# Seven-product units four tiles earlier, with the weight sums moved and the last tile's left half stored on its own

## The chip, the cores and the metric

The kernel runs on one core of one Trainium2 chip. The metric is the time of one launch in device microseconds, as the median of seven runs. TensorE (PE in the profile) multiplies matrices, VectorE (DVE), ScalarE (ACT) and GpSimd (POOL) work element by element, SyncE (SP) issues most transfers. Matrix results arrive in PSUM, in eight banks of 512 fp32 columns for each of 128 partitions; everything else lives in SBUF.

## The reference

Linear attention with a cosine weighting, and then a gated feed-forward block:

```python
# q, k, v: 8 batches x 8 heads x 576 positions x 64
phi(x)  = concat(relu(x) * cos_w, relu(x) * sin_w)            # 128 features
kv      = einsum('bhsf,bhsd->bhfd', phi(k), v)
z       = sum over s of phi(k)
x       = einsum(phi(q), kv) / (einsum(phi(q), z) + 1e-6)     # -> 4608 tokens x 512
out     = (gelu(x @ w_gate) * (x @ w_val)) @ w_out            # 512 -> 1536 -> 512
```

## The kernel before, in words

The 4608 tokens are nine blocks of 512, numbered 0 to 8, and the 1536 hidden columns are twelve tiles of 128 (`JT`). A **unit** is one tile of one block: gate and value for it, the gelu, and the product that gives a tile of `hT`. The attention of batch n + 1 (`kv_unit`, and then five `nm_unit`s that give the numerators and `x_sb`) is spread over the units of block n, and `turn_x` transposes `x_sb` into `xT` by transfers on SyncE's queue.

For blocks 1 to 6 a unit is `gv_unit` (line 401): four matmuls of 128 x 512 for the gate and four for the value, a gelu on ScalarE (line 409) and a multiply on VectorE (line 410). For blocks 7 and 8 it is `fast_unit` (line 602). There gate and value are the two rows of a 2 x 2 block product of W and x, halved along the contraction and along the tokens, and are computed with seven half-size products (`GV`, Winograd's form of Strassen's scheme), each of two matmuls of 128 x 256. It needs four sums of weight blocks, S1 to S4 (`w_sum`, line 566, in slices of 512 columns, 128 x 1024 elements for an instruction), and four sums of x blocks for each block of tokens, T1 to T4 (`x_sum`, line 582). `wa["S1"]` and `wa["S2"]` lie in buffers named `qf`, S3 in `kf`, S4 in `vf`, and the T's in `qp`, whose earlier contents are no longer wanted. In the trace a matmul `ps<-qp,qf` is therefore a product of T and S. Within a unit, product 6 accumulates onto the bank of product 1 and so waits for ScalarE's copy of product 1 (line 631); product 4 accumulates onto product 7's bank and waits for VectorE's reading of it (line 637). Products 7 and 4 of unit t - 1 are issued within unit t.

The output product of block n - 1 runs between the units of block n: it too is in seven products (`product`, line 510, six matmuls of 128 x 256 each), with sums of `hT` blocks (`h_sum`, line 494). VectorE makes these sums up to block 6's units; in the `fast_unit` stretch GpSimd makes them. Each unit of the stretch takes the output step of the unit before it (`o_step`), so the first has none. A finished tile of 128 rows is stored by `store` (line 421) as two transfers of 64 rows.

The order on each engine is the program's order (`tc.manual_schedule()`): an engine stops at an instruction that waits, and all behind it wait too. Before the change the regimes meet at `FAST`, counted in blocks, and the sums have fixed places among the units of block 6:

```python
FAST = NB - 2
W_SUMS = {0: (0,), 1: (1,), 7: (2, 3, 4), 8: (5, 6), 9: (7, 8), 10: (9, 10), 11: (11,)}
...
            if n == FAST - 1:
                for i in W_SUMS.get(jt, ()):
                    w_sum(f"S{i // 3 + 1}", 512 * (i % 3), 512 * (i % 3) + 512)
                if jt >= 8:
                    x_sum(FAST, jt - 8)
```

After the last unit come the output products of block 8's last two tiles of rows, p = 0 and p = 1, in an order written out by hand; the last are product 4 and product 3 of p = 1, which finish the tile `hi` (tokens 384 to 511 of the block) and the right half of `lo` (tokens 128 to 255).

Of the kernel before, what the change touches and what calls it, by code (L numbers as in the profile page):

```python
# [16 lines left out]
def kernel(  # L17
# [13 lines left out]
    nc = tc.nc  # L31

    B, H, S, D = q.shape
    F = 2 * D
    C = H * D
    J = moe_w_gate.shape[1]
    CT = C // 128
    JT = J // 128
    NP = H // 2
    R = S // 64  # L40
    NB = B * S // 512
# [90 lines left out]
    for i in range(2):  # L132
        t = consts.tile([128, NP, R, D + 1], BF16, name=f"vx{i}")
# [282 lines left out]
    def store(engs, i, o_sb, c0=0, c1=C):  # L416

        for n, eng in enumerate(engs):
            b, j = divmod(2 * i + n, R)
            dst = out[b * S:(b + 1) * S, c0:c1].rearrange("(p j) c -> j p c", j=R)[j]  # L420
            eng.dma_start(out=dst, in_=o_sb[64 * n:64 * n + 64, c0:c1])

    def flush(engs=(nc.sync, nc.sync)):
        for i, o_sb in stores:
            store(engs, i, o_sb)
        stores.clear()
# [22 lines left out]
    JH, CH = JT // 2, C // 2  # L449
# [53 lines left out]
    def product(n, p, i, u, m, v):  # L503


        a, b = PROD[i]
        key = n, p
        at = {1: u, 6: u, 7: u, 5: m, 3: m, 2: v, 4: v}[i]
        for j in range(JH):
            nc.tensor.matmul(  # L510
                at,
                lhsT=hs.setdefault(key, h_parts(n, p))[a][:, j],
                rhs=ts[b][:, j],
                start=(j == 0 and i in (1, 2, 4, 5)),
                stop=(j == JH - 1),
                skip_group_check=i in (3, 6, 7),
            )
        if key not in got:
            got[key] = [outp.tile([128, C], FP32, name="o_sb") for _ in range(2)]
        lo, hi = got[key]  # L520
        last = n == NB - 1

        def add(o, k, x, op=ALU.add):
            nc.vector.tensor_tensor(o, got[key, k], x, op=op)  # L524

        if i in (1, 6, 7) or last and i == 5:
            got[key, i] = place(n, p, f"u{i}", CH, FP32)
            nc.scalar.copy(got[key, i], at)  # L528
        if i == (2 if last else 1):
            add(lo[:, LEFT], 1, v)  # L530
        if i == 7:
            add(hi[:, RIGHT], 7, got[key, 5] if last else m)
        if i == 4:
            add(hi[:, LEFT], 7, v, ALU.subtract)
        if i == 3:
            add(lo[:, RIGHT], 6, m)
        if i in (3, 4):
            flush()
            stores.append((4 * n + 2 + p, hi) if i == 4 else (4 * n + p, lo))
            if last:  # L540
                flush((nc.sync, nc.scalar if p == 1 else nc.sync))

# [1 line left out]

    FAST = NB - 2
    CP = CT // 2  # L550
    wa, xb, temps = {}, {}, {}

    def w_sum(name, j0, j1):
        if not wa:
            wa["A11"], wa["A12"] = wg_sb[:, 0:CP], wg_sb[:, CP:CT]
            wa["A21"], wa["A22"] = wv_sb[:, 0:CP], wv_sb[:, CP:CT]
        if name not in wa:
            was = {"S1": "qf", "S2": "qf", "S3": "kf", "S4": "vf"}[name]
            wa[name] = inp.tile([128, CP, J], BF16, name=was)
        x, y, op = {  # L560
            "S1": ("A21", "A22", ALU.add),
            "S2": ("S1", "A11", ALU.subtract),
            "S3": ("A11", "A21", ALU.subtract),
            "S4": ("A12", "S2", ALU.subtract),
        }[name]
        nc.vector.tensor_tensor(  # L566
            wa[name][:, :, j0:j1], wa[x][:, :, j0:j1], wa[y][:, :, j0:j1], op=op
        )

    def x_sum(n, i):  # L570
        if n not in xb:
            xt = xT[n]
            xb[n] = {
                "B11": xt[:, 0:CP, 0:256], "B12": xt[:, 0:CP, 256:512],
                "B21": xt[:, CP:CT, 0:256], "B22": xt[:, CP:CT, 256:512],
            }
        if "x" not in temps:
            temps["x"] = attn.tile([128, 2, 4, CP, 256], BF16, name="qp")
        b = xb[n]
        x, y = (("B12", "B11"), ("B22", "T1"), ("B22", "B12"), ("B21", "T2"))[i]  # L580
        b[f"T{i + 1}"] = temps["x"][:, n - FAST, i]
        nc.vector.tensor_tensor(b[f"T{i + 1}"], b[x], b[y], op=ALU.subtract)  # L582

    GV = {
# [5 lines left out]
    def fast_unit(t, between):  # L590


        def at(i, t):
            if i == 2:
                return ps[:, 0, 256 * (t % 2):256 * (t % 2) + 256]
            return bank((3, 1)[t % 2] if i in (3, 5) else (2, 6, 7)[t % 3])[:, 0:256]

        def mm(i, t):
            n, jt = FAST + t // JT, t % JT
            a, b = GV[i]  # L600
            for ct in range(CP):
                nc.tensor.matmul(  # L602
                    at(i, t),
                    lhsT=wa[a][:, ct, jt * 128:(jt + 1) * 128],
                    rhs=xb[n][b][:, ct],
                    start=(ct == 0 and i in (1, 5)),
                    stop=(ct == CP - 1),
                    skip_group_check=i not in (1, 5),
                )

        def tmp(i, t):
            if "t" not in temps:
                temps["t"] = attn.tile([128, 6, 256], FP32, name="qT")
            return temps["t"][:, 2 * i + t % 2]

        def h(t, half):
            n, jt = FAST + t // JT, t % JT
            if n not in hT:
                hT[n] = ffn.tile([128, JT, BLK], BF16, name="hT")
            return hT[n][:, jt, 256 * half:256 * half + 256]  # L620

        def gelu(t, half, src):
            if t not in gels:
                gels[t] = ffn.tile([128, BLK], FP32, name="gel")
            nc.scalar.activation(gels[t][:, 256 * half:256 * half + 256], src, AF.Gelu)

        new, old = t < 2 * JT, t > 0
        M5, U6, G2 = range(3)
        if new:
            mm(1, t)  # L630
            nc.scalar.copy(at(2, t), at(1, t))  # L631
            mm(5, t)
            nc.scalar.copy(tmp(M5, t), at(5, t))
        if old:
            mm(7, t - 1)
            gelu(t - 1, 1, tmp(G2, t - 1))
            nc.vector.tensor_tensor(at(3, t - 1), tmp(M5, t - 1), at(7, t - 1), op=ALU.add)
            nc.vector.tensor_tensor(
                h(t - 1, 1), gels[t - 1][:, 256:512], at(3, t - 1), op=ALU.mult
            )  # L640
        between()
        if new:
            mm(6, t)
            nc.scalar.copy(tmp(U6, t), at(6, t))
            mm(2, t)
            gelu(t, 0, at(2, t))
            mm(3, t)
            nc.vector.tensor_tensor(tmp(G2, t), tmp(U6, t), at(3, t), op=ALU.add)
        if old:
            mm(4, t - 1)  # L650
            nc.vector.tensor_tensor(
                h(t - 1, 0), gels[t - 1][:, 0:256], at(4, t - 1), op=ALU.mult
            )
# [186 lines left out]
    for n in range(4, 8):  # L840
        SUMS[n] = {0: "1", 1: "23", 2: "4", 3: "5", 4: "6", 5: "7", 6: "8"}

    W_SUMS = {0: (0,), 1: (1,), 7: (2, 3, 4), 8: (5, 6), 9: (7, 8), 10: (9, 10), 11: (11,)}


    q3 = {
# [5 lines left out]
        (2, 1): ((8,), ()),  # L852
    }
    turn[0] = 1
    for n in range(1, FAST):
        b = n + 1

        t_kv, t_nm, t_turn = {1: (7, 9, 12), 2: (6, 7, 11), 3: (2, 5, 9)}.get(n, (1, 2, 8))
        for jt in range(JT):
            if n == 1 and jt >= t_nm:  # L860
                nm_unit(2, jt - t_nm, (6, 4, 6)[jt - t_nm])
                turn_x(2, jt - t_nm)
# [64 lines left out]
                        turn_x(c, i)  # L927
            if n == 1 and 4 <= jt < 8:
                wo_sum(f"T{jt - 3}")
            if n == FAST - 1:  # L930
                for i in W_SUMS.get(jt, ()):
                    w_sum(f"S{i // 3 + 1}", 512 * (i % 3), 512 * (i % 3) + 512)
                if jt >= 8:
                    x_sum(FAST, jt - 8)


    def o_step(n, jt):
        p, u = divmod(jt, 6)
        for i in ((2, 1), (5,), (6,), (7,), (4,), (3,))[u]:
            product(n - 1, p, i, ps[:, 4, 0:CH], ps[:, 5, 0:CH], ps[:, 4, CH:C])  # L940
        for i in map(int, SUMS[n].get(jt, "")):
            h_sum(n - 1, i // 5, f"S{(i - 1) % 4 + 1}", eng=nc.gpsimd)
        if jt % 3 == 1:
            flush()

    for t in range(2 * JT):
        n, jt = FAST + t // JT, t % JT
        if n == NB - 1 and jt in (9, 10):
            h_sum(n, jt - 9, "S3", eng=nc.gpsimd)
        fast_unit(t, lambda: o_step(FAST + (t - 1) // JT, (t - 1) % JT) if t else None)  # L950
        if (n, jt) == (NB - 1, JT - 2):
            for name in ("S1", "S2", "S4"):
                h_sum(n, 0, name, 0, JH - 2, eng=nc.gpsimd)
        if n == FAST and jt in (2, 4, 6, 8):
            x_sum(NB - 1, jt // 2 - 1)

    def last_product(p, i, to=0):
        product(
# [4 lines left out]
        o_step(NB - 1, JT - 1)  # L963
        last_product(0, 1)

    fast_unit(2 * JT, ends)


    for what in (
# [38 lines left out]
```

## Time and profile before

| what | value |
|---|---|
| median of 7 runs | 316.08 us (315.38 to 316.92) |
| the profiled execution's own time | 315.34 us |
| its span | 313.6 us |
| TensorE busy | 303.8 us |
| VectorE, ScalarE, GpSimd busy | 248.0, 183.2, 59.1 us |
| last matmul ends | 308.7 us from the span's start |
| first `fast_unit` matmul | 242.0 us |

The profile is of one execution. Its page gives busy times by engine, then the chain of work that ended last, followed back from the last instruction, and groups of instructions by line with their mean durations. The trace behind it answers for any stretch: a timeline lists start, duration, engine, line and operands, and in brackets the idle time of that engine just before and what ended it. A matmul's duration reaches from its start to its modelled end, and matmuls overlap, so their cost on TensorE is the spacing of starts, which the chain shows.

### The profile page before, as it was taken

Reading aid. Unit: us, or ns where it says so; the run is one execution under the profiler, and the core shown is the slowest. Engines: PE = TensorE matmul, PEld = TensorE weight load, DVE = VectorE, ACT = ScalarE, POOL = GpSimd, SP = SyncE. Lnnn points to the kernel's source line nnn. Section 1 sums busy time; section 2 is a strip of 40 time slices with the busy share of each in tenths; the row PEclk is TensorE's granted clock in tenths of the full one; section 3 lists DMA queues with packets and bytes.
Section 4 is the critical chain, followed back from the end, with each engine's and each line's share of the span. In section 5 each row is a group of like instructions: output and inputs, shape, how many; then the busy total and the mean of one; then the engine's idle time right before and its main releaser. Section 6 shows DMA issues by size and latency. Waiting matters only on the chain.

```text
span 313.6 us, 7631 instructions
## 1 busy us (share of the span) xinstructions
PE 303.8 (97%) x2871; PEld 205.9 (66%) x2871; DVE 248.0 (79%) x610; ACT 183.2 (58%) x452; POOL 59.1 (19%) x64
## 2 busy tenths in 40 slices
PE   8899999999999999999999999999999899999993
PEld 3574456655866676665665666656665688888883
DVE  5864696699897996798697959887889998878782
ACT  7864676957475754366427732683223587777841
POOL 6584420000000000000000000000000951297310
PEclk9999999999999999999999999999999999999999
DMA  7999999861798946984896699365441102113025
GB/s 265 257 183 249 310 320 413 257 151 41 227 216 296 313 97 173 369 183 121 300 294 102 147 323 262 68 120 116 95 92 32 38 10 61 43 27 70 2 68 134
DMA packets 68949, 53.65 MB, mean 171 GB/s; under 512 B 45360, under 2 KB 54064, under 8 KB 68912
## 3 DMA queue, kind: packets, MB, share of 16 engines
q1 hardware_dynamic: 59104, 41.10, 49.7%
q0 software_dynamic: 9648, 11.80, 16.2%
q8 instruction: 22, 0.36, 0.5%
q10 hardware_dynamic: 160, 0.26, 0.2%
q14 instruction: 15, 0.12, 0.1%
HBM read 37.75 MB, written 9.44 MB: 150 GB/s over the span
## 4 chain that ended last, share of the span: by engine, by line
PE 90%; DVE 4%; DMA 3%; issue 1%; SPq 1%; ACT 0%; DVEq 0%
PE ps L401 44%; PE ps L510 23%; PE ps L602 11%; PE ps L431 3%; PE ps L283 3%; PE ps L242 3%; DMA vf<-in_v_dram 3%; DVE qp L582 1%; PE ps L205 1%; PE ps L373 1%; PE ps L358 1%; SPq L81 1%; DVE o_sb L524 0%; DVE vf L566 0%; DVE hT L410 0%
## 5 line engine op out<-in xcount | busy, mean ns | idle before, releaser
L401 PE MATMUL ps<-xT,wg_sb 128*128 128x512 bf16 (+1 forms) x360 | 85.6, 360 | 0.0
L401 PE MATMUL ps<-xT,wv_sb 128*128 128x512 bf16 (+1 forms) x360 | 85.6, 360 | 0.0
L409 ACT ACTIVATE gel<-ps 128x512 f32<-128x512 f32 (+1 forms) x90 | 50.2, 559 | 51.1 <-PE ps L401 44.5
L410 DVE TENSOR_TENSOR hT<-gel,ps 128x512 bf16<-128x512 f32 (+1 forms) x90 | 56.9, 636 | 26.2 <-PE ps L401 21.3
L401 PEld LDWEIGHTS <-wv_sb 128*128 128x128 bf16 x360 | 35.2, 98 | 35.8
L494 POOL TENSOR_TENSOR S<-hT 128x768 bf16<-128x768 bf16 x8 | 13.3, 1663 | 212.1 <-DVE hT L410 199.0
L401 PEld LDWEIGHTS <-wg_sb 128*128 128x128 bf16 x360 | 32.3, 98 | 21.9 <-issue 0.2
L510 PEld LDWEIGHTS <-S 128*128 128x128 bf16 x336 | 32.9, 98 | 11.5 <-DVE S L494 0.7
L528 ACT COPY u<-ps 128x256 f32<-128x256 f32 x42 | 15.6, 372 | 33.5 <-PE ps L510 33.0
L510 PE MATMUL ps<-T,S 128*128 128x256 bf16 x252 | 34.4, 273 | 0.0
L161 ACT ACTIVATE qp<-qf,sin_t 128x256 bf16<-128x256 f32 x72 | 32.1, 502 | 2.0 <-DMA qf<-in_q_dram 2.0
L510 PEld LDWEIGHTS <-hT 128*128 128x128 bf16 x288 | 28.2, 98 | 7.1
L524 DVE TENSOR_TENSOR o_sb<-u,ps 128x256 f32<-128x256 f32 x56 | 23.4, 417 | 12.0 <-ACT u L528 11.5
L161 ACT ACTIVATE kp<-kf,sin_t 128x256 bf16<-128x256 f32 (+1 forms) x73 | 30.0, 480 | 0.9 <-DMA kf<-in_k_dram 0.9
L296 DVE TENSOR_TENSOR x_sb<-ps,rec 128x512 bf16<-128x512 f32 x38 | 26.3, 691 | 1.7 <-DMA xT<-x_sb 0.4
L510 PE MATMUL ps<-wo_sb,hT 128*128 128x256 bf16 x192 | 23.7, 273 | 0.0
L163 DVE TENSOR_SCALAR qp<-qf,cos_t 128x256 bf16<-128x256 f32 x71 | 21.6, 351 | 2.7 <-DMA qf<-in_q_dram 2.7
L602 PE MATMUL ps<-qp,qf 128*128 128x256 bf16 x96 | 18.3, 272 | 0.3 <-ACT ps L631 0.3
L602 PE MATMUL ps<-xT,wg_sb 128*128 128x256 bf16 x96 | 18.3, 273 | 0.0
L163 DVE TENSOR_SCALAR kp<-kf,cos_t 128x256 bf16<-128x256 f32 x63 | 18.3, 348 | 0.0
L283 PEld LDWEIGHTS <-qT 128*128 128x128 bf16 x304 | 14.6, 98 | 2.6 <-ACT qT L698 0.3
L283 PE MATMUL ps<-kv_sb,qT 128*128 128x65 bf16 x304 | 16.1, 194 | 0.0
(117 smaller groups left out, 416.1 us busy)
## 6 DMA issues: line engine op xcount, KB each, us to landing
out_dram<-o_sb SPq DMA_DIRECT2D x70, 128.0 KB, 2.4
kf<-in_k_dram SPq DMA_DIRECT2D x12, 576.0 KB, 6.9
vf<-in_v_dram SPq DMA_DIRECT2D x12, 576.0 KB, 8.9
qf<-in_q_dram SPq DMA_DIRECT2D x10, 576.0 KB, 4.9
qf<-in_q_dram POOLq DMA_DIRECT2D x4, 576.0 KB, 12.2
kf<-in_k_dram POOLq DMA_DIRECT2D x4, 576.0 KB, 12.6
vf<-in_v_dram POOLq DMA_DIRECT2D x4, 576.0 KB, 12.7
wg_sb<-in_moe_w_gate_dram POOLq DMA_DIRECT2D x6, 256.0 KB, 6.1
```

What stands on the lines that cost most here:

```text
L161: nc.scalar.activation(o, i, AF.Relu, scale=tab[:, j:j + 1])
L163: (eng or nc.vector).tensor_scalar(o, i, 0.0, tab[:, j:j + 1], op0=ALU.max, op1=ALU.mult)
L283: nc.tensor.matmul(bank(b0 + h // 4)[:, (h % 4) * (D + 1):(h % 4 + 1) * (D + 1)], lhsT=q_cols(b, t, h), rhs=kv_sb[b][:, h // 2, h % 2, :], ...
L296: nc.vector.tensor_tensor(x, nm[:, :, :, 0:D], rec[:, :, :, None].to_broadcast([128, 2, 4, D]), op=ALU.mult,)
L401: nc.tensor.matmul(bank(b0 + g)[:, 0:w], lhsT=wt[:, ct, js], rhs=xt[:, ct, c0:c0 + w], start=(ct == 0), stop=(ct == CT - 1),)
L409: nc.scalar.activation(gel[:, 0:w], bank(b0)[:, 0:w], AF.Gelu)
L410: nc.vector.tensor_mul(hT[n][:, jt, c0:c0 + w], gel[:, 0:w], bank(b0 + 1)[:, 0:w])
L494: eng.tensor_tensor(a[name][:, j0:j1], a[x][:, j0:j1], a[y][:, j0:j1], op=op)
L510: nc.tensor.matmul(at, lhsT=hs.setdefault(key, h_parts(n, p))[a][:, j], rhs=ts[b][:, j], start=(j == 0 and i in (1, 2, 4, 5)), stop=(j == ...
L524: nc.vector.tensor_tensor(o, got[key, k], x, op=op)
L528: nc.scalar.copy(got[key, i], at)
L602: nc.tensor.matmul(at(i, t), lhsT=wa[a][:, ct, jt * 128:(jt + 1) * 128], rhs=xb[n][b][:, ct], start=(ct == 0 and i in (1, 5)), stop=(ct == ...
```

## The change

The boundary is now counted in units: the last four units of block 6 (8 to 11) are done by `fast_unit` as well, 28 of them instead of 24. During these four the output step keeps its own unit's place, and the first unit of block 7 has no output step; from then on each takes the step of the unit before, as it was.

The W sums are split by columns. Those for columns 1024 to 1535, which the four new units use, and all of S1 and S3 are made by VectorE, from block 5 on. The first two thirds of S2 and S4 are made by GpSimd, 128 x 1024 elements for an instruction, after a copy of one element of block 7's T4 into `gate`; the copy stands ahead of them in GpSimd's order. The x sums of block 6 (new) go to its units 3 to 6, those of block 7 to its unit 7, those of block 8 to units 8 to 11 of block 7. In block 6 the remaining transposes of x go to unit 7 instead of unit 8.

In the last tile pair (p = 1 of block 8), the left half of `lo` is stored after product 2, by two transfers on SyncE's queue; `hi` after product 4, on SyncE's and GpSimd's; the right half of `lo` after product 3, on SyncE's and ScalarE's. Before, `hi` and the whole of `lo` were stored on SyncE's and ScalarE's queues. The pending stores are flushed once more after the last unit.

```diff
-        if i in (3, 4):
+        if last and p == 1:
+            if i == 2:
+                store((nc.sync, nc.sync), 4 * n + p, lo, 0, CH)
+            if i == 4:
+                store((nc.sync, nc.gpsimd), 4 * n + 2 + p, hi)
+            if i == 3:
+                store((nc.sync, nc.scalar), 4 * n + p, lo, CH, C)
+        elif i in (3, 4):
             flush()
             stores.append((4 * n + 2 + p, hi) if i == 4 else (4 * n + p, lo))
             if last:
-                flush((nc.sync, nc.scalar if p == 1 else nc.sync))
+                flush()
...
-    FAST = NB - 2
+    FAST = (NB - 3) * JT + 8
+    UNITS = NB * JT - FAST
...
-    def w_sum(name, j0, j1):
+    def w_sum(name, j0, j1, eng=nc.vector):
...
-        nc.vector.tensor_tensor(
+        eng.tensor_tensor(
...
-        b[f"T{i + 1}"] = temps["x"][:, n - FAST, i]
+        b[f"T{i + 1}"] = temps["x"][:, n % 2, i]
...
-    W_SUMS = {0: (0,), 1: (1,), 7: (2, 3, 4), 8: (5, 6), 9: (7, 8), 10: (9, 10), 11: (11,)}
+    MORE = {
+        (5, 0): [("S1", 0, 512)], (5, 1): [("S1", 512, 1024)],
+        (5, 8): [("S3", 0, 512)], (5, 9): [("S3", 512, 1024)],
+        (6, 0): [("S1", 1024, J), ("S2", 1024, J)],
+        (6, 1): [("S3", 1024, J)], (6, 2): [("S4", 1024, J)],
+        (6, 3): [(6, 0)], (6, 4): [(6, 1)], (6, 5): [(6, 2)], (6, 6): [(6, 3)],
+        (6, 7): [(7, 0), (7, 1), (7, 2), (7, 3)],
+        (7, 8): [(8, 0)], (7, 9): [(8, 1)], (7, 10): [(8, 2)], (7, 11): [(8, 3)],
+    }
+
+    def more(n, jt):
+        for what in MORE.get((n, jt), ()):
+            (w_sum if len(what) == 3 else x_sum)(*what)
...
-    for n in range(1, FAST):
+    for n in range(1, NB - 2):
...
+        if n == 6:
+            t_turn = 7
-        for jt in range(JT):
+        for jt in range(min(JT, FAST - n * JT)):
...
-    for t in range(2 * JT):
-        n, jt = FAST + t // JT, t % JT
+    for t in range(UNITS):
+        n, jt = divmod(FAST + t, JT)
...
-        fast_unit(t, lambda: o_step(FAST + (t - 1) // JT, (t - 1) % JT) if t else None)
+        if n < NB - 2:
+            fast_unit(t, lambda: o_step(n, jt))
+            if t == 0:
+                nc.gpsimd.tensor_copy(gate, xb[NB - 2]["T4"][:, CP - 1, 255:256])
+            a, j0 = (("S2", 0), ("S4", 0), ("S2", 512), ("S4", 512))[t]
+            w_sum(a, j0, j0 + 512, eng=nc.gpsimd)
+        elif (n, jt) == (NB - 2, 0):
+            fast_unit(t, lambda: None)
+        else:
+            fast_unit(t, lambda: o_step(*divmod(FAST + t - 1, JT)))
+        more(n, jt)
...
-    fast_unit(2 * JT, ends)
+    fast_unit(UNITS, ends)
+    flush()
```

More of the change, by code (lines that the diff above doesn't have):

```diff
@@ L616, in h @@
         def h(t, half):
-            n, jt = FAST + t // JT, t % JT
+            n, jt = divmod(FAST + t, JT)
             if n not in hT:
@@ L625, in gelu @@
             nc.scalar.activation(gels[t][:, 256 * half:256 * half + 256], src, AF.Gelu)
-        new, old = t < 2 * JT, t > 0
+        new, old = t < UNITS, t > 0
         M5, U6, G2 = range(3)
@@ L929 @@
                 wo_sum(f"T{jt - 3}")
[L930 to L934, printed above, removed]
+            more(n, jt)
     def o_step(n, jt):
@@ L944, in o_step @@
             flush()
-    for t in range(2 * JT):
-        n, jt = FAST + t // JT, t % JT
+    for t in range(UNITS):
+        n, jt = divmod(FAST + t, JT)
         if n == NB - 1 and jt in (9, 10):
             h_sum(n, jt - 9, "S3", eng=nc.gpsimd)
-        fast_unit(t, lambda: o_step(FAST + (t - 1) // JT, (t - 1) % JT) if t else None)
+        if n < NB - 2:
[8 more added lines that the diff above has]
+            fast_unit(t, lambda: o_step(*divmod(FAST + t - 1, JT)))
+        more(n, jt)
         if (n, jt) == (NB - 1, JT - 2):
@@ L953 @@
                 h_sum(n, 0, name, 0, JH - 2, eng=nc.gpsimd)
-        if n == FAST and jt in (2, 4, 6, 8):
-            x_sum(NB - 1, jt // 2 - 1)
     def last_product(p, i, to=0):
```

## The prediction

> **What bounds the kernel now.** I read the page's busy table, the chain that ended last, then the timelines of each engine around the change from full products to seven products, the groups by form, and the stores at the end. A unit is one column tile (0 to 11) of a block of 512 tokens (0 to 8); t counts seven-product units.
>
> ```profile
> PE 303.8 (97%) x2871; PEld 205.9 (66%) x2871; DVE 248.0 (79%) x610; ACT 183.2 (58%) x452; POOL 59.1 (19%) x64
> PE 90%; DVE 4%; DMA 3%; issue 1%; SPq 1%; ACT 0%; DVEq 0%
> ```
>
> TensorE bounds it: only fewer matmul slots, fewer gaps, or a shorter end can move the time. The chain, in order of time (start, us, what):
>
> ```profile
> 232.66 1.73 PE ps L401 x8
> ...
> 245.09 1.85 DVE qp L582
> ...
> 249.63 1.53 PE ps L602 x14
> 251.16 0.66 PE ps L510 x6
> ```
>
> A full unit is 8 matmuls in 1.73 us, a seven-product unit 14 in 1.53; six matmuls of the output product (0.66 or 0.65) stand between. Between the two regimes the chain leaves TensorE for VectorE. The timelines of PE, DVE and POOL there:
>
> ```profile
> 242.90 0.38 PE L602 MATMUL ps<-qp,qf 128*128 128x256 bf16 x2 [0.28 <-ACT ps L631]
> ...
> 247.85 0.38 PE L602 MATMUL ps<-qp,wv_sb 128*128 128x256 bf16 x2 [1.52 <-DVE ps L637]
> ```
>
> ```profile
> 243.13 2.03 DVE L566 TENSOR_TENSOR vf<-wg_sb,qf 128x1024 bf16<-128x1024 bf16 x1
> 245.09 1.85 DVE L582 TENSOR_TENSOR qp<-xT,qp 128x512 bf16<-128x512 bf16 x1
> ```
>
> ```profile
> 242.98 1.63 POOL L494 TENSOR_TENSOR S<-hT 128x768 bf16<-128x768 bf16 x1 [199.04 <-DVE hT L410]
> 244.69 1.96 POOL L494 TENSOR_TENSOR S<-S,hT 128x768 bf16<-128x768 bf16 x1
> ```
>
> The reader sees two sums on VectorE three to four times their usual length (the same forms take 0.69 and 0.42 us), exactly while GpSimd sums, and TensorE waiting behind them. The bracketed idle understates it, since the last matmul's drain counts as busy. I count slots: from 242.02 (first seven-product matmul) to 251.65 there are 44 matmuls of gate and value and 24 of output, 68 x 0.109 = 7.42 us, in 9.63 us. **The change of regime costs 2.21 us**: 0.44 at the first wait, 1.68 at the second, 0.09 after it.
>
> [...] the sums above grew by 1.34 and 1.43 us, while the operations that take one input from PSUM stayed at 0.42 us beside the same GpSimd sums. [...] The stores here land after 2.2 to 3.0 us; no small store from GpSimd is in this trace.
>
> **Part 1, four more units in seven products.** Units 8 to 11 of block 6: 32 matmuls at 0.216 (6.91 us) become 56 at 0.109 (6.12): **-0.79 us**, all on the path, since TensorE has no idle there. Beside it ScalarE gets five 0.36 to 0.43 us operations a unit for one of 0.60, and VectorE four of 0.42 for one of 0.68. The existing seven-product stretch carries just that beside gapless TensorE, so it costs nothing; without that cover each late VectorE step would hold fourth products as at 247.85.
>
> **Part 2, the sums.** Twelve W sums of 0.69 us ran on VectorE in block 6; now eight run there from block 5 on, four on GpSimd. One more set of four x sums (0.42 each, about 0.35 apart) is added for block 6. I laid these into VectorE's timeline. Block 5, units 8 and 9: +1.2 us, into idle pieces of 1.33 and 0.66 us; unit 0 of block 6 gets two W sums for one (+0.6), into 1.52 us of idle before unit 2's multiply. Units 3 to 6 get one x sum each, so a unit needs 0.60 + 0.33 + 0.47 + 1.05 + 0.35 = 2.8 us against 2.64 on TensorE: VectorE falls behind by up to 0.8 us and catches up in the 0.95 us of idle before 230.46. The tightest place is the numerators: their banks 6 and 7 must be read before the next eight matmuls. Those at 226.72 follow an x_sb which ended at 226.25 and would end at 226.6: 0.1 us to spare. Cost taken 0, bounds 0 and +0.5; it cannot be below 0, as there is no idle there to win. Block 7's four x sums follow unit 7's multiply, 233.3 to 234.9.
>
> GpSimd's four sums are held by a one-element copy from the last of these, so they meet no two-SBUF-input operation of VectorE: during t = 0 to 3 its operands come from PSUM and one SBUF tile. No 128x1024 sum on GpSimd is in the trace; the rows by form are
>
> ```profile
> L494 POOL TENSOR_TENSOR S<-hT 128x768 bf16<-128x768 bf16 x8 | 13.3, 1663 | 212.1 <-DVE hT L410 199.0 <-PE ps L602 12.5 <-PE ps L510 0.6
> L494 POOL TENSOR_TENSOR kf<-hT 128x512 bf16<-128x512 bf16 x1 | 1.2, 1154 | 4.9 <-DVE hT L638 4.9
> ```
>
> The unstretched 1.64 and 1.15 us give 1.9 ns an element, so 2.1 us for 1024. From 235.1 they end at 237.2, 239.4, 241.5 and 243.7. Unit t starts at 232.5 + 2.19 t: S2's first half is needed at 241.9, S4's at 242.3, the second halves four units later. Queued behind them on GpSimd is the first sum S1 of block 6's h, whose last operand comes at about 243.6; it ends at 245.3 and is needed at 246.5. Cost taken 0; with the worst stretch seen (1.96/1.63) a sum is 2.6 us and that product waits 0.6. Bounds 0 and +0.6.
>
> **Part 3, the change of regime.** The 2.21 us go, as no VectorE sum overlaps a GpSimd one and block 7's x sums are done ten microseconds before use. At t = 0 the six output matmuls now stand ahead of product 6 and cover ScalarE's copy. At t = 4 (unit 0 of block 7) nothing does: only product 7 of the unit before precedes, so product 6 issues 0.66 us after the unit's start where the copy is done at 0.88 (242.02 to 242.90 before). That leaves 0.22: **-1.99 us** (bounds -2.2 and -1.4). The transposes of block 8's x move one unit earlier in SyncE's queue, past no store that delays anyone: 0.
>
> **Part 4, the end.** The last stores' issues (start, us):
>
> ```profile
> 309.15 0.54 SPq L421 DMA_DIRECT2D out_dram<-o_sb  x1
> 309.25 0.73 ACTq L421 DMA_DIRECT2D out_dram<-o_sb  x1
> ```
>
> Both carry 128 KB and follow VectorE's last add (308.70 to 309.12). Now they carry 64 KB, ScalarE's queue no longer issues the other tile's half before (about 0.1 us), and 128 KB less are moved in all[...]. The left half's two issues go earlier, at about 301 us, ahead of two stores of the first tile that nobody waits for. In exchange half a tile goes through GpSimd at about 305.8: 0.7 to 0.8 us to issue (its load rows) for 0.56[...], so it lands about when the last one does. Taken **-0.3 us**; bounds -0.7 and +0.3.
>
> **Sum.** -0.79 - 1.99 - 0.30 = -3.1 us. The profiled execution took 315.34 us (span 313.6 and 1.74 around it), so 312.2, with a span of 310.5 and the last matmul ending near 305.9 instead of 308.7. That execution lies 0.74 under the median of 316.08; the median becomes **313.0 us**.
>
> **Rivals.** (A) VectorE becomes the bound: the numerators' 0.1 us is not enough, or the four x sums of block 7 push t = 0's work, so that stalls of 1 to 2 us come back in block 6. For it: a demand of 2.8 against 2.64 us. Against: 0.95 us of idle right after. Half the gain or less, 314.5 us. (B) Slower: GpSimd paces the start of block 7. If a W sum takes d, the four end at 235.1 + 4d and S1 1.64 later, needed at 246.5: every 0.1 us of d beyond 2.44 costs 0.4 us. From d = 3.2 the whole gain is gone; at 3.6 TensorE loses 4.6 us, net +1.5, 317.6. For it: the size isn't in the trace and strides over two runs of 512. Against: the straight line through two sizes, and no contention. (C) The GpSimd store lands last by 1 us: the tail turns to +0.7, 314.0. (D) The change doesn't hold GpSimd back: excluded, since the copy reads what the last x sum writes, and stands first in GpSimd's order.
>
> **The numbers.** Forecast 0.74, all of it faster; A 0.14 (0.08 faster, 0.05 same, 0.01 slower); B 0.07 (0.02 same, 0.05 slower); C 0.05, faster. A measurement of this kernel can tell about 0.3% (0.95 us) from no change. Faster 0.87, same 0.07, slower 0.06. The bounds of parts 1 to 4, each taken on one side, add up to -3.7 (312.4) and -0.8 (315.3); that all four fall on the bad side is as unlikely as B. With the spread of 1.5 us among the runs shown, and with A and C inside, the range is 312.1 to 314.9; B and the worst of A, about 0.12, and some 0.05 below lie outside.
>
> **What would show it.** Right: TensorE's group of 128x512 falls by 32 and that of the seven products grows by 56; all W and x sums on VectorE at 0.69 and 0.42; four GpSimd sums near 2.1 us ending before 244; one gap of some 0.2 us at t = 4; landing within 2.8 us of the last add. Wrong: waits of TensorE on DVE in units 3 to 7 of block 6 (A), on POOL at t = 4 or 6 (B), or the GpSimd store as the last to land (C).

## The result and the profile after

| what | before | after |
|---|---|---|
| median | 315.84 us (31 runs) | 313.31 us (12 runs) |
| profiled execution, its span | 315.34, 313.6 us | 313.48, 311.7 us |
| TensorE busy | 303.8 us | 302.6 us |
| last output matmuls start | 307.85 us | 305.83 us |

The ratio is 0.9923, with a 95% interval of 0.9908 to 0.9937: 2.4 us faster, clear of noise, inside the stated range of 312.1 to 314.9.

The two spans differ by 1.9 us only, so the first question is how much of that is the change. The chain of after, around the change of regime (start, us, what):

```profile
227.50 0.33 PE ps L283 x8
...
233.50 0.44 PE ps L611 x4
233.94 0.66 PE ps L510 x6
234.60 1.31 PE ps L611 x12
...
240.93 1.11 PE ps L611 x10
...
242.11 0.36 ACT ps L640
...
242.52 1.69 PE ps L611 x14
```

The chain stays on TensorE where it left for VectorE before. At 233.94 the output step stands between the first products of the new units; the one break is at 242.11, unit 0 of block 7, where ScalarE's copy is not covered. The eight numerator matmuls at 227.50 took 0.33 us instead of 0.26: the tight place of the prediction, 0.07 us late.

VectorE's timeline shows block 7's x sums at their usual length, and GpSimd's shows its four W sums after the holding copy:

```profile
234.54 0.42 DVE L591 TENSOR_TENSOR qp<-xT,qp 128x512 bf16<-128x512 bf16 x1
...
235.22 0.42 DVE L591 TENSOR_TENSOR qp<-xT,qp 128x512 bf16<-128x512 bf16 x1
```

```profile
235.71 0.17 POOL L974 CAST gate<-qp 128x1 f32<-128x1 bf16 x1 [190.36 <-DVE qp L591]
235.90 2.13 POOL L575 TENSOR_TENSOR qf<-qf,wg_sb 128x1024 bf16<-128x1024 bf16 x1
...
242.40 2.13 POOL L575 TENSOR_TENSOR vf<-wg_sb,qf 128x1024 bf16<-128x1024 bf16 x1
244.49 1.64 POOL L494 TENSOR_TENSOR S<-hT 128x768 bf16<-128x768 bf16 x1
```

To compare TensorE without what comes earlier, I take the stretch from the first matmul of the last `kv_unit` (block 6, unit 1) to the start of the last group of output matmuls. Those rows, from the timelines of PE, are for before and then for after

```profile
214.98 1.33 PE L242 MATMUL ps<-vx,kp 64*128 64x65 bf16 x72
...
307.85 0.82 PE L510 MATMUL ps<-wo_sb,vf 128*128 128x256 bf16 x6
```

```profile
215.76 1.33 PE L242 MATMUL ps<-vx,kp 64*128 64x65 bf16 x72
...
305.83 0.82 PE L510 MATMUL ps<-wo_sb,vf 128*128 128x256 bf16 x6
```

that is 92.87 us against 90.07, **2.80 us less**. Of the 0.78 us by which this profile is late at 215.76, 0.76 are already there at the third batch's `kv_unit` (70.16 against 69.40), far ahead of the first changed instruction.

At the end, after's timeline of the stores' queues:

```profile
306.83 0.56 POOL L421 DMA_DIRECT2D out_dram<-o_sb  x1 [9.11 <-DVE o_sb L524]
...
307.14 0.56 ACTq L421 DMA_DIRECT2D out_dram<-o_sb  x1
```

VectorE's last add ends at 307.10, the span 4.6 us later; before it was 309.12 and 4.5 us. The tail shows no gain here.

### The profile page after: what moved, and what is told of

It is laid out like the page before. It is cut to its first block, busy times and chain, and to the rows that moved or that the text cites. A ratio compares the mean times of both kernels' runs of the same rounds, so it can differ in the third digit from the quotient of the medians.

```text
span 311.7 us, 7732 instructions
## 1 busy us (share of the span) xinstructions
PE 302.6 (97%) x2895; PEld 208.0 (67%) x2895; DVE 246.4 (79%) x622; ACT 186.8 (60%) x468; POOL 68.7 (22%) x70
## 4 chain that ended last, share of the span: by engine, by line
PE 77%; DMA 14%; issue 4%; POOL 2%; DVE 1%; SPq 0%; ACT 0%; POOLq 0%; DVEq 0%; ACTq 0%
PE ps L401 38%; PE ps L510 20%; PE ps L611 13%; DMA qf<-in_q_dram 8%; PE ps L283 3%; DMA wv_sb<-in_moe_w_val_dram 2%; PE ps L242 2%; DMA vf<-in_v_dram 2%; DMA wg_sb<-in_moe_w_gate_dram 1%; POOL kf L494 1%; PE ps L431 1%; SPq L81 0%; PE ps L358 0%; POOL gate L679 0%; POOL qf L81 0%
## 5 line engine op out<-in xcount | busy, mean ns | idle before, releaser
L401 PE MATMUL ps<-xT,wg_sb 128*128 128x512 bf16 (+1 forms) x344 | 81.5, 359 | 0.0
L401 PE MATMUL ps<-xT,wv_sb 128*128 128x512 bf16 (+1 forms) x344 | 81.4, 359 | 0.0
L409 ACT ACTIVATE gel<-ps 128x512 f32<-128x512 f32 (+1 forms) x86 | 47.8, 557 | 46.3 <-PE ps L401 41.9
L410 DVE TENSOR_TENSOR hT<-gel,ps 128x512 bf16<-128x512 f32 (+1 forms) x86 | 54.1, 634 | 21.9 <-PE ps L401 19.0
L401 PEld LDWEIGHTS <-wv_sb 128*128 128x128 bf16 x344 | 33.6, 98 | 33.9
L401 PEld LDWEIGHTS <-wg_sb 128*128 128x128 bf16 x344 | 30.7, 98 | 20.9 <-issue 0.3
L611 PE MATMUL ps<-qp,qf 128*128 128x256 bf16 x112 | 21.4, 272 | 0.1
L611 PE MATMUL ps<-xT,wg_sb 128*128 128x256 bf16 x112 | 21.4, 273 | 0.0
```

Of the source, the lines that this page charges most:

```text
L401: nc.tensor.matmul(bank(b0 + g)[:, 0:w], lhsT=wt[:, ct, js], rhs=xt[:, ct, c0:c0 + w], start=(ct == 0), stop=(ct == CT - 1),)
L409: nc.scalar.activation(gel[:, 0:w], bank(b0)[:, 0:w], AF.Gelu)
L410: nc.vector.tensor_mul(hT[n][:, jt, c0:c0 + w], gel[:, 0:w], bank(b0 + 1)[:, 0:w])
L611: nc.tensor.matmul(at(i, t), lhsT=wa[a][:, ct, jt * 128:(jt + 1) * 128], rhs=xb[n][b][:, ct], start=(ct == 0 and i in (1, 5)), stop=(ct == ...
```

## The experiments

All in one table first; the stretch is the one just defined, the tail goes from the end of VectorE's last add to the end of the span, both from the profiled execution.

| kernel | median (before on its chip) | ratio to before, 95% | stretch | tail |
|---|---|---|---|---|
| before | 315.84 | | 92.87 | 4.5 |
| after | 313.31 (315.84) | 0.9923 (0.9908 to 0.9937) | 90.07 | 4.6 |
| after again | 312.96 (316.31) | 0.9900 (0.9884 to 0.9916) | 90.07 | 4.5 |
| stores as before | 313.68 (316.31) | 0.9919 (0.9905 to 0.9933) | 90.07 | 5.2 |
| the same, again | 313.72 (315.83) | 0.9926 (0.9907 to 0.9945) | 90.07 | 4.4 |
| half of lo early, nothing on GpSimd | 312.48 (316.31) | 0.9887 (0.9869 to 0.9905) | 90.08 | 3.9 |
| the same, again | 312.63 (315.83) | 0.9903 (0.9886 to 0.9920) | 90.07 | 3.9 |
| whole lo late, hi's half on GpSimd | 313.15 (315.83) | 0.9919 (0.9904 to 0.9934) | 90.08 | 4.8 |
| sums moved only, 24 units | 314.65 (316.31) | 0.9953 (0.9939 to 0.9967) | 91.01 | 4.5 |
| held by an earlier sum | 323.15 (316.11) | 1.0211 (1.0180 to 1.0243) | 98.96 | 4.6 |
| not held | 318.04 (316.11) | 1.0056 (1.0038 to 1.0075) | 90.07 | 4.6 |
| one W sum twice on GpSimd | 315.37 (316.11) | 0.9974 (0.9962 to 0.9987) | 91.58 | 4.7 |
| best | 312.38 (316.11) | 0.9875 (0.9853 to 0.9898) | 89.85 | 3.9 |

**After again.** No edit.

> The changed kernel once more, for direct comparison with the others of this set, and for a second profile. The profile of it showed TensorE 0.8 us later than the kernel before already ahead of any changed instruction. Theory 1 (that lag is chance in the load phase): ratio to before 0.990 to 0.993, and block 5 starts at another time in this profile. Theory 2 (the change itself delays the first 200 us): the same lag of 0.7 to 0.9 us again.

The third batch's `kv_unit` starts at 69.33 in this profile, at 70.16 in the first, and between 69.2 and 70.5 in those of the kernels that follow, whose load phase is the same; the lag is chance in the load phase. Block 5, to which W sums were moved, takes no longer for them: from its `kv_unit` to block 6's it is 32.55 us before and after.

**Sums moved only.** The boundary is put back to block 7; all sums stay on VectorE.

```diff
-    FAST = (NB - 3) * JT + 8
+    FAST = (NB - 2) * JT
...
-        (6, 3): [(6, 0)], (6, 4): [(6, 1)], (6, 5): [(6, 2)], (6, 6): [(6, 3)],
-        (6, 7): [(7, 0), (7, 1), (7, 2), (7, 3)],
+        (6, 7): [("S2", 0, 512)], (6, 8): [("S2", 512, 1024), (7, 0)],
+        (6, 9): [("S4", 0, 512), (7, 1)], (6, 10): [("S4", 512, 1024), (7, 2), (7, 3)],
```

> Seven products from block 7 on, as before, but with all W and x sums on VectorE and done ahead of GpSimd's first sum; the tail as changed. Only part 3 of the prediction is left. Prediction's theory: of the 2.21 us at the change of regime 1.77 go (0.44 stays, ScalarE's copy uncovered at the first unit), so 1.8 us faster than before, and 1.0 us slower than the changed kernel (0.79 for the four units, 0.21 for that wait). Rival (the 2.21 us come from the change of regime as such, not from the overlap of sums): hardly faster than before, 2.5 us slower than the changed kernel.

```profile
243.85 0.38 PE L611 MATMUL ps<-qp,qf 128*128 128x256 bf16 x2 [0.28 <-ACT ps L640]
```

The stretch is 1.86 us shorter than before; the only wait left among TensorE's matmuls there is ScalarE's copy at the first unit, shown by its timeline. W and x sums took 0.68 and 0.42 us on VectorE. So 1.86 of the 2.80 us come from moving the sums out of GpSimd's way, and 0.94 from the four units with the wait they help cover. The rival falls. This run also gives VectorE less to do at the change of regime; that it is the overlap that counts, the next run shows. No run has the four units with all sums on VectorE, so whether GpSimd's share of them was needed stays open.

**Held by an earlier sum.** GpSimd is released by block 6's last x sum instead of block 7's.

```diff
-                nc.gpsimd.tensor_copy(gate, xb[NB - 2]["T4"][:, CP - 1, 255:256])
+                nc.gpsimd.tensor_copy(gate, xb[NB - 3]["T4"][:, CP - 1, 255:256])
```

> The changed kernel, but GpSimd's four W sums are released by block 6's T4 instead of block 7's, about 2 us earlier, so that they run beside VectorE's four x sums of block 7. Prediction's theory (two-SBUF-input sums of VectorE and GpSimd's sums shut each other out): each x sum takes about as long as a GpSimd sum, 2.1 us instead of 0.42, unit 0's add G2 comes some 6 us late and TensorE waits for it at product 4 of the first seven-product unit: 4 to 7 us slower than the changed kernel, 317 to 320. Rival (VectorE was late before only because it had too much to do): the same as the changed kernel, x sums of 0.42 us.

Rows of the timelines of DVE, POOL and PE, in three fences, and then the stretches with their granted clock (us, then busy time and count of PE, PEld, DVE, ACT, POOL, then PEclk, DMA share, GB/s):

```profile
234.67 2.16 DVE L591 TENSOR_TENSOR qp<-xT 128x512 bf16<-128x512 bf16 x1
...
241.26 2.33 DVE L591 TENSOR_TENSOR qp<-xT,qp 128x512 bf16<-128x512 bf16 x1
```

```profile
234.42 2.12 POOL L575 TENSOR_TENSOR qf<-qf,wg_sb 128x1024 bf16<-128x1024 bf16 x1
...
241.13 2.17 POOL L575 TENSOR_TENSOR vf<-wg_sb,qf 128x1024 bf16<-128x1024 bf16 x1
```

```profile
244.51 0.59 PE L611 MATMUL ps<-qp,wv_sb 128*128 128x256 bf16 x2 [6.70 <-DVE ps L646]
```

```profile
237.80:244.50 6.70, 0.00 (x1) 0.00 (x0) 6.55 (x5) 0.55 (x2) 5.43 (x3) 0.80 0.00 0
244.50:246.00 1.50, 1.49 (x8) 1.06 (x8) 1.41 (x4) 1.06 (x5) 0.00 (x0) 0.50 0.00 0
246.00:248.00 2.00, 2.00 (x11) 1.45 (x10) 1.16 (x3) 0.67 (x2) 0.00 (x0) 0.50 0.01 4
248.00:250.00 2.00, 2.00 (x17) 1.64 (x16) 1.07 (x4) 1.35 (x5) 0.00 (x0) 0.83 0.32 75
```

Each of VectorE's four sums starts at most 0.3 us after a GpSimd sum and ends some 0.3 us after that one's end: 2.2 to 2.3 us for a 0.42 us operation. The same work moved by 2 us turns a gain into a loss. Both expectations were too low for its size: the stretch is 8.9 us longer, of which 6.9 are the gap between the starts of third and fourth products less one slot, and 2.0 that TensorE came back at half its clock: from 244.51 to 248.72 it issued 20 matmuls in 4.21 us instead of 2.19. The granted clock was 0.50 in both stretches up to 248.00, 0.83 in the next and 1.00 from 250 to 254. Around the shorter waits of 1.52 us before the change and of 1.95 us in the next run the stretches show 1.00; how long a wait lowers it no run shows.

**Not held.** The copy is left out.

```diff
-            if t == 0:
-                nc.gpsimd.tensor_copy(gate, xb[NB - 2]["T4"][:, CP - 1, 255:256])
```

> The changed kernel without the holding copy. GpSimd's W sums then start as soon as S1 and the buffers are there, around 203 us, in units 8 to 11 of block 5. Prediction's theory: two W sums and some others on VectorE stretch there by 1.3 to 2.1 us each, but VectorE has some 2 us of idle around and TensorE 3 us before a bank is missed: within 0.5 us of the changed kernel. Rival (any overlap of the two engines costs TensorE its length): 2 to 4 us slower.

GpSimd did start at 204.68. The rows of DVE's and PE's timelines:

```profile
206.03 5.25 DVE L163 TENSOR_SCALAR kp<-kf,cos_t 128x256 bf16<-128x256 f32 x3
```

```profile
212.53 1.02 PE L401 MATMUL ps<-xT,wv_sb 128*128 128x512 bf16 x4 [1.95 <-DVE hT L410]
...
215.86 0.94 PE L510 MATMUL ps<-wo_sb,hT 128*128 128x256 bf16 x7 [1.76 <-DVE hT L410]
```

My expectation missed, and so did its rival: from block 5's `kv_unit` to block 6's it took 37.29 us, 4.7 more, and then 90.07 as after. The W sums of VectorE, which the expectation named, did not stretch; what did are the preparations of k. These have one tensor input, and it and the output are in SBUF; three of them took 5.25 us for the 0.87 they take before, up to 211.28, beside GpSimd sums that began at 204.68, 206.88 and 208.96 and took 2.12 to 2.17 us. The multiply behind them came 4.4 us late, and TensorE missed a bank and then the tile of `hT`. At 211.20 it was the other way round: a W sum of VectorE that started 0.01 us before GpSimd's last one took its usual 0.68 us, and GpSimd's took 2.65 instead of 2.12. In these five pairs, this one and the four of the run before (VectorE 0.13 to 0.25 us behind), the one that started later was stretched more.

**One W sum twice on GpSimd.**

```diff
-            w_sum(a, j0, j0 + 512, eng=nc.gpsimd)
+            for _ in range(2 if t == 3 else 1):
+                w_sum(a, j0, j0 + 512, eng=nc.gpsimd)
```

> The changed kernel with the last of GpSimd's four W sums made twice: 2.15 us more ahead of block 6's first h sum. In the profile after, that sum ends at 246.13 and its product is issued at 246.88, so 0.75 us are free. Theory B of the prediction: 2.15 - 0.75 = 1.4 us slower than the changed kernel (ratio 1.0045 to it), and a wait of TensorE on POOL of 1.4 us. Rival (later sums catch up or the product has more room): under 0.5 us.

```profile
247.96 0.83 PE L510 MATMUL ps<-T,S 128*128 128x256 bf16 x6 [1.33 <-POOL S L494]
```

PE's timeline has the wait where it was said to be, and the stretch is 1.51 us longer. The first h sum ended 2.19 us later, so the slack of GpSimd in the changed kernel is about 0.7 us, and what went beyond it here was lost in full. By the ratios the run is 1.6 or 2.3 us slower than the change, as one takes the change's first or second set.

**The stores, four combinations.** Three edits beside the change itself: the old code; hi's second half on ScalarE; and lo whole at the end with hi's second half on GpSimd.

```diff
-                store((nc.sync, nc.gpsimd), 4 * n + 2 + p, hi)
+                store((nc.sync, nc.scalar), 4 * n + 2 + p, hi)
```

> The changed kernel with the stores of the kernel before: hi and the whole of lo at the end, on SyncE and ScalarE. Prediction's theory: the split tail is worth 0.3 us, so this is 0.3 us slower than the changed kernel, 313.6. Rival (the store through GpSimd gives back what the halved last store wins, as the profile after suggests, 4.6 us from the last add to the end against 4.5 before): the same as the changed kernel within 0.15 us, span from the last add to the end 4.5 us.

> The changed kernel with the second half of hi on ScalarE's queue instead of GpSimd's; lo still in halves. If the store through GpSimd is what gives the win back: 0.3 to 0.5 us faster than the changed kernel (about 312.9), 4.1 to 4.2 us from the last add to the end. If GpSimd costs nothing and halving the last store brings nothing either: the same within 0.15 us.

> The stores of the kernel before once more, since the earlier profile of it had one store that took 3.8 us to land. If that was chance: 4.5 us from the last add to the end of the span, and 0.0 to 0.3 us slower than the changed kernel's 313.0. If two 128 KB stores on each of two queues land late as a rule: 5 us and more again, 0.6 us slower.

> Half of lo early and nothing through GpSimd, once more. If the store through GpSimd costs 0.7 us at the end: 3.9 us from the last add to the end of the span again, against 4.6 of the changed kernel, and about 0.5 us faster than it.

> The whole of lo at the end, as before, but hi's second half through GpSimd, as changed: the fourth of the four combinations. If halving and GpSimd add up (halving -0.7, GpSimd +0.7): about 5.2 us from the last add to the end, the slowest of the four, 0.6 us slower than the changed kernel. If GpSimd's queue is simply the last to be done and hides lo: 4.6 us, the same as the changed kernel.

What SyncE's queue waits for at the end, of after and then of the variant on ScalarE (us in total, times, longest):

```profile
SPq L1033 <- DMA out_dram<-o_sb: 2.3, 2, 1.2
SPq L1033 <- PEq L1033: 1.0, 2, 0.5
```

```profile
SPq L1033 <- DMA out_dram<-o_sb: 1.9, 2, 1.5
SPq L1033 <- PEq L1033: 0.7, 2, 0.5
```

With ScalarE the tail is 3.9 us in both profiles (and in the best version), with GpSimd 4.5 to 4.7 in the six that have it beside a halved lo. So halving lo wins 0.6 us against the kernel before (4.5), GpSimd's store costs 0.7, and they nearly cancel. SyncE waits 0.4 us less for the stores on ScalarE and 0.3 us less in the closing sequence. The last stores' times from issue to landing, of after and then of the variant on ScalarE (KB each, us):

```profile
out_dram<-o_sb POOLq DMA_DIRECT2D x1, 128.0 KB, 2.9
out_dram<-o_sb SPq DMA_DIRECT2D x1, 64.0 KB, 2.8
out_dram<-o_sb ACTq DMA_DIRECT2D x1, 64.0 KB, 2.9
```

```profile
out_dram<-o_sb SPq DMA_DIRECT2D x1, 64.0 KB, 2.3
out_dram<-o_sb ACTq DMA_DIRECT2D x1, 64.0 KB, 2.5
```

GpSimd's store, issued 0.3 us ahead of ScalarE's, also lands 0.3 us ahead of it: it is not itself the last, but beside it the halves of lo take 0.4 to 0.5 us longer. Why, and why the closing sequence grows with it, no run shows.

The two effects don't simply add up. The fourth combination gave 4.8 us, between its two expectations: with lo whole, GpSimd's store costs 0.3 to 0.4 us against the tails of 4.5 and 4.4, and nothing against that of 5.2. The ratios of the two ScalarE runs lie below those of the stores as before (0.9887 and 0.9903 against 0.9919 and 0.9926), though neighbouring intervals touch or overlap. In the first run of the old code, with its tail of 5.2 us, all four of the last stores took 3.5 to 3.8 us to land, where the second's took 2.3 to 3.0; what delayed them is not known. So what the tail as changed is worth against the old one stays open: 4.5 to 4.7 us against 4.4, 4.5 and 5.2 in the profiles, and 312.96 against 313.68 us by the medians on one chip, with overlapping intervals.

**Best.** hi on ScalarE's queue; the last output step of block 6 cut into two halves of three matmuls, around units 11 and 0; S4's last VectorE sum one unit earlier.

```diff
-            fast_unit(t, lambda: o_step(n, jt))
+            fast_unit(t, lambda: o_step(n, jt) if t < 3 else half(0, JH // 2))
...
-            fast_unit(t, lambda: None)
+            fast_unit(t, lambda: half(JH // 2, JH))
```

> The changed kernel with the second half of hi on ScalarE's queue, the last output step of block 6 split into three and three matmuls over units 11 and 0 so that ScalarE's copy is covered at unit 0 of block 7, and S4's last W sum one unit earlier. Expected: the wait of 0.23 us at unit 0 gone, the 0.07 us at the numerators gone, end of the last add to end of span 3.9 us: 0.9 us faster than the changed kernel, of which 0.3 show in TensorE from unit 1 of block 6 to the end. Rival (with a shorter cover unit 11 waits instead): 0.6 us faster.

Its chain:

```profile
227.76 0.33 PE ps L283 x8
...
240.53 0.33 PE ps L510 x3
240.86 1.53 PE ps L613 x14
242.39 0.33 PE ps L510 x3
242.72 1.53 PE ps L613 x14
```

Three matmuls cover the copy on both sides and the wait is gone; the stretch is 89.85 us, 0.22 less. The 0.07 us at the numerators stayed, so moving S4's sum did nothing for them. With the shorter tail it is the fastest of all by its median and its ratio; against the changed kernel's own second run (0.9900) the intervals overlap slightly, and against the variant on ScalarE (0.9887) largely, so that the gain of 0.22 us rests on the stretch alone.

## Why the prediction was right, point by point

- **The bound.** Right: TensorE's slots and gaps moved the time; added work on the other engines cost nothing as long as no wait reached TensorE (block 5, with its W sums, 32.55 us before and after).
- **Part 1, -0.79 us, and the covered copy.** Predicted 1.00 us between "sums moved only" and the change; measured 0.94, with the 0.07 us that the numerators lost inside it (all groups of eight took 0.26 with the sums moved only). TensorE's group of full products fell by 32 matmuls and that of the seven products grew by 56, as said; the slots of 0.216 and 0.109 us in the working are the chain's 1.73/8 and 1.53/14, where a 128x256 matmul is recorded with 0.27: the bracketed idle time is shorter than the counted one by the difference, 0.16.
- **Part 2, 0.** The 0.1 us to spare at the numerators was -0.07. A GpSimd W sum took 2.13 us against 2.1 by the line through two sizes. With this profile's lag of 0.78 us taken off, GpSimd kept the times worked out: its sums began at 235.12 (235.1) and block 6's first h sum ended at 245.35 (245.3). TensorE, though, was there at 246.10 instead of 246.5. The working gave each new unit 2.19 us, but the first one, which has no unit before it whose products 7 and 4 it could take, lasted 1.75 (233.34 to 235.09). So the slack was 0.75 us for 1.2. Doubling a sum confirmed rival B's price (1.5 us for 1.4) and with it how near the change is to that edge.
- **Part 3, -1.99.** Right in cause and nearly in size: -1.86 with sums moved alone, where 1.77 was worked out, and the remaining wait at unit 0 was 0.23 for 0.22. The 0.09 us more lie just behind the stretch that was counted: before, block 8's first x sum (251.06) met a GpSimd sum too, took 0.85 us, and TensorE's matmul at 252.83 came 0.09 us late; in the changed kernel every x sum takes 0.42. Parts 1 to 3 gave 2.80 for 2.78. That they agree so closely is partly luck, as this 0.09 and the numerators' 0.07, neither of which is in the sum, nearly cancel. That the overlap of sums is the cause was shown by making it come back.
- **Part 4, -0.3.** The term that was mis-sized is GpSimd's store. Its issue took 0.56 us, and it landed about when the last one does, as forecast, but it was priced at next to nothing, and by the profiles it costs 0.7 us; halving lo wins 0.6. Of the -0.3 the timeline of before gives about 0.1, ScalarE's issue of the other tile's half; the rest was my estimate, which no trace shows. The sum is within the stated bounds, and by the profiles close to none; by the medians on one chip it may be more than -0.3. The sign "landing within 2.8 us of the last add" was just missed, with 2.9.
- **Rivals.** A did not appear beyond 0.07 us. B is real 0.7 us further on. C came true in its effect and not in its way: the store takes back the tail's gain, without turning it into a loss, but it does not land last. D is out: the copy began at 235.71, after block 7's last x sum (235.22 and 0.42 us long), and the sums behind it; without the copy they began at 204.68.
- **The sum.** -3.1 us against -2.4 (ratio 0.9923) and -3.2 (0.9900) in two sets of runs. Their profiles differ by 0.83 us in the load phase (70.16 against 69.33) and by nothing in the stretch, so a part of the total as small as part 4 cannot be read from these times.

## What to carry to other kernels

Before work is given to GpSimd, list what VectorE runs at that time. Beside GpSimd's W sums its x sums, with two inputs in SBUF, went from 0.42 us to between 2.16 and 2.33, and three `tensor_scalar`s from SBUF to SBUF from 0.87 to 5.25; its operations with one input in PSUM and one in SBUF stayed at 0.41 to 0.43 (128x256, beside the W sums of the changed kernel). Release GpSimd by the last result of an operation that was stretched so and that VectorE still has to make; the one-element copy did that here in 0.17 us. When products are put ahead or behind, keep something on TensorE's queue between an operation and the one that waits for another engine's copy: three matmuls of 0.11 us on each side were enough here for a wait of 0.23 us. Measure a stretch between two fixed instructions, not the span, when the gain is as small as what the load phase scatters.

## What the runs showed of the hardware that I had not expected

- VectorE's `tensor_scalar` from fp32 in SBUF was stretched beside GpSimd's sums, as two-input sums were: 5.25 us for three, 0.87 without. Where VectorE's sum started first, by 0.01 us, GpSimd's was stretched instead, to 2.65 us from 2.12.
- After 6.7 us without a matmul TensorE was granted half its clock (0.50 from 244.50 to 248.00), and 2.0 us more were lost on top of the wait.
- A store through GpSimd's queue among the last ones lengthened the end by 0.7 us beside two 64 KB stores (0.3 to 0.4 us beside two of 128 KB), though it was issued 0.3 us before the last of them and also landed before it.
